# Ranks, expert choice, weight splits and the first slots' x in the attention half of an attention and mixture-of-experts kernel

## The chip, the core and the metric

The kernel runs on one core of a Trainium2 chip. The metric is device time in microseconds. Three runs of the kernel before took 625.83, 627.03 and 627.37 us; the median is 627.03 us.

## What is computed

Windowed attention (each position sees itself and the 63 before it) for 8 batches, 8 heads, 576 positions of 64 features gives 4608 tokens of 512 features. Each token then goes to one of 8 experts, and is scaled by its gate. All data is float32.

```python
scores = scale * np.matmul(q, k.transpose(0, 1, 3, 2))        # then mask, softmax
x = np.matmul(attn, v)  # as (4608, 512)

xn = x / (np.linalg.norm(x, axis=-1, keepdims=True) + 1e-06)
en = expert_emb / (np.linalg.norm(expert_emb, axis=-1, keepdims=True) + 1e-06)
logits = xn @ en.T / tau
expert_idx = np.argmax(logits, axis=1)
gate_w = probs[np.arange(N), expert_idx]                       # probs: softmax of logits
for e in range(E):
    mask = expert_idx == e
    h = np.maximum(x[mask] @ w1[e], 0.0)
    out[mask] = gate_w[mask, None] * (h @ w2[e])
```

## The kernel before

**Attention.** The 4608 tokens are 36 tiles of 128 rows. `stages(s)` (L520) is one turn of a software pipeline, called for s = 0 to 34: it computes the scores of tile s, the weights times values of tile s-2, and the transposed x and the logits of earlier tiles. The order of the work on each engine is the order in which this code stands; a wait on one instruction holds all that is queued behind it on that engine. In a stage ACT copies the scores out of PSUM (`own_scores`, L222), DVE puts the previous block's scores in (`all_scores`, L225) and takes maxima (L229), POOL subtracts them (`less_max`, L233), ACT takes the exponential (L236), PE transposes, ACT copies (L255), DVE and POOL mask the two halves (L258 and L261), PE multiplies with the values (L275 and L289), and DVE divides by the sums (`x_out`, L313 to L315).

**Routing.** Tiles form groups of four up to tile 28 and of two behind it (`GROUPS`, L33). Logits of a group land in PSUM (`misc`) and are copied beside x into the group's rows in SBUF (`four_out`, L361; L545; `logits_out`, L378). `choose(G)` (L382) takes the first largest of the eight logits of each token in five DVE steps (L391 to L395), three stages behind the group's end: for the groups of four in stages 7, 11, 15, 19, 23, 27 and 31. Two stages later, in 9, 13, 17, 21, 25, 29 and 33, `ranks(G)` (L407) lets PE sum how many earlier tokens chose each expert, with matmuls of bfloat16 ones. `rank_rows` (L440) then adds on DVE each expert's first row in the table (`at`: a constant, or `late0`, `late1` behind the cuts at tiles 20 and 32), multiplies with the choice, sums over experts and converts: the row in which the token's x goes. `place(T)` (L459) is the put: POOL issues an indirect DMA (L462) that writes the tile's rows into the table `xs` in DRAM, one in most stages.

**Slots.** Behind the attention, `step(g)` works through slots of 128 rows of one expert, two to a full group, with both layers in three float32r products of split operands: high part by ACT, rest by DVE or POOL. The first four slots are expert 0's earliest tokens, known before the attention ends. `load_x(a)` (L750) reads slot a's rows from `xs` with four DMAs on SP's queue into `xb`; for slots 0 and 1 it stands behind stage 30, behind that stage's put. `x_turned` (L763) transposes blocks of 32 on DVE (L770, four rows `x4`), `x_hi` (L779) rounds on ACT (L781), `x_lo` (L783) subtracts on POOL (L785). `x_parts` does the three in a row; for slots 0 and 1 behind stages 32 and 33.

**Weights.** Expert 0's w1 is loaded during the attention in eight halves of `w1raw` (L508), by stages 8, 10, 15, 18, 21, 24, 26 and 28. `wsplit` (L513) names the stages at whose end a half is split: ACT rounds it (L600), DVE subtracts (L601), stages 13, 15, 20, 23, 26, 28, 30 and 32. Halves of w2 are loaded in stages 29 to 33 (L512).

**The end of the attention.** The last tile and the first slots' first layer are interleaved by hand (L1082 to L1227): `layer1(0, f)` on PE between the last stages' work, the last ranks, `load_x(2)` and `load_x(3)`, then `slot_rows` (L652), a chain of small DVE steps that finds the expert and first row of every later slot, and the loads that depend on it.

Lines that the change touches and the prediction names are given with the numbers of the kernel before.

Of the kernel before, what the change touches and what calls it, by code (L numbers as in the profile page):

```python
# [9 lines left out]
F32 = mybir.dt.float32  # L10
# [5 lines left out]
ALU = mybir.AluOpType  # L16
# [5 lines left out]
P = 128  # L22
B, H, S, D = 8, 8, 576, 64
N, DM, DF, E = 4608, 512, 1024, 8
# [12 lines left out]
CUTS = 20, 32  # L37
# [18 lines left out]
K_ID, K_OWN, K_PREV, K_SEL, K_E, K_DESC, K_P, K_F, K_SL, K_U = 0, 128, 256, 384, 448, 456, 464, 465, 473, 476  # L56
# [27 lines left out]
def attention_moe(ctx, tc, q, k, v, emb, tau, w1, w2, kc, kt, out):  # L84
    nc = tc.nc
    ctx.enter_context(tc.manual_schedule())
    const = ctx.enter_context(tc.tile_pool(name="const", bufs=1))
# [53 lines left out]
    upper = const.tile([P, P], BF16, name="upper")  # L141
    ones = const.tile([P, P], BF16, name="ones")
    half = const.tile([P, 1], F32, name="half")
    embT = ap.tile([P, 4, 32], F32, name="embT", bufs=1)
    xs = dram.tile([TBL, ROW], F32, name="xs")

# [27 lines left out]
    def load_k(T, engine=nc.sync):  # L174
        if T < NT:
            engine.dma_start(kT[:, T % RK * KT:(T % RK + 1) * KT], k[T])
# [195 lines left out]
    def in_rows(G):  # L372

        return x_rows(*GROUPS[G])[:, :, C_LOG:C_LOG + E]
# [6 lines left out]

    def choose(G):  # L382

        L = in_rows(G)
        a, b = GROUPS[G]
        n = b - a
        m = ap.tile([P, n, 1], F32, name="m")
        c8 = ap.tile([P, n, E], F32, name="c8")
        oh = ohs[G] = ap.tile([P, n, E], BF16, name="oh")
        sh = [P, n, E]  # L390
        nc.vector.reduce_max(out=m, in_=L, axis=AX.X)  # L391
        nc.vector.tensor_tensor(out=c8, in0=L, in1=m.to_broadcast(sh), op=ALU.is_equal)
        nc.vector.tensor_tensor(out=c8, in0=c8, in1=cs[:, K_DESC:K_DESC + E].unsqueeze(1).to_broadcast(sh), op=ALU.mult)
        nc.vector.reduce_max(out=m, in_=c8, axis=AX.X)
        nc.vector.tensor_tensor(out=oh, in0=c8, in1=m.to_broadcast(sh), op=ALU.is_equal)  # L395
# [11 lines left out]
    def ranks(G):  # L407

        a, b = GROUPS[G]
        n = b - a  # L410
        rank[G] = rkb[0][:, 64:128].rearrange("p (a g e) -> p a g e", a=2, e=E)[:, G % 2, :n]
        nc.tensor.matmul(rank[G], lhsT=upper, rhs=ohs[G], start=True, stop=False)
        for i in range(1, n):
            nc.tensor.matmul(rank[G][:, i:], lhsT=ones, rhs=ohs[G][:, i - 1:i].to_broadcast([P, n - i, E]), start=False, stop=False)
        for i in range(4):
            nc.tensor.matmul(rank[G], lhsT=ones, rhs=before[G][:, i:i + 1].to_broadcast([P, n, E]), start=False, stop=i == 3)

    late = [const.tile([P, E], F32, name=f"late{i}") for i in range(len(CUTS))]
    shift = [const.tile([P, 1], F32, name=f"shift{i}") for i in range(len(CUTS))]
# [20 lines left out]
    def rank_rows(G):  # L440
        a, b = GROUPS[G]
        n = b - a
        rk = ap.tile([P, n, E], F32, name="rk")
        at = [cs[:, K_E:K_E + E], *late][sum(a >= cut for cut in CUTS)]
        nc.vector.tensor_tensor(out=rk, in0=rank.pop(G), in1=at.unsqueeze(1).to_broadcast([P, n, E]), op=ALU.add)
        yield
        nc.vector.tensor_tensor(out=rk, in0=rk, in1=ohs.pop(G), op=ALU.mult)
        yield
        pos = ap.tile([P, n], F32, name="pos")
        nc.vector.reduce_sum(out=pos, in_=rk, axis=AX.X)  # L450
        yield
        rks[G] = ap.tile([P, n], I32, name="pi")
        nc.vector.tensor_copy(rks[G], pos)
        yield
# [4 lines left out]
    def place(T):  # L459

        i = T - GROUPS[OF[T]][0]
        d = nc.gpsimd.indirect_dma_start(  # L462
            out=xs[:, :], out_offset=bass.IndirectOffsetOnAxis(ap=rks[OF[T]][:, i:i + 1], axis=0),
            in_=xr.pop(T), in_offset=None, bounds_check=TBL - 1, oob_is_err=False)
        d = getattr(d, "ins", d)
        for o in firsts:
            tc.declare_no_dep(d, o, reason="later tokens' places are behind the early slots")
        for o in puts:
            tc.declare_no_dep(d, o, reason="no two tokens share a place")
        puts.append(d)  # L470
# [39 lines left out]
    for i, s0 in enumerate((29, 30, 30, 31, 31, 32, 32, 33)):  # L510
        c, h = divmod(i, 2)
        wsteps.setdefault(s0, []).append(lambda c=c, h=h: nc.sync.dma_start(out=w2raw[c][:, h], in_=w2v[0, :, c, h]))  # L512
    wsplit = {s0: (i // 2, slice(i % 2 * 512, i % 2 * 512 + 512)) for i, s0 in enumerate((13, 15, 20, 23, 26, 28, 30, 32))}  # L513

    def warm(n, to=back):

# [3 lines left out]
    def stages(s):  # L520

        def there(d):
            return 0 <= s - d < NT

        def ending(d):
            return [G for G, (a, b) in enumerate(GROUPS) if b + d == s]

        def turned():
            if there(1):
                attn_transposes(s - 1)  # L530
                attn_copy(s - 1)

        scores(s)
        if s < 3:
            warm(12, misc)
        own_scores(s)
        if there(4) and s - 4 >= 28:
            logits(s - 4)
        four = [G for G in ending(3) if len(range(*GROUPS[G])) == 4]
        for G in ending(3):  # L540
            if G in four:
                logits_four(G)
                four_copy(G)
            else:
                nc.scalar.copy(in_rows(G), plv[:, G % 2, :GROUPS[G][1] - GROUPS[G][0]])  # L545
        load_q(s + RQ)
        if there(2):
            values_other(s - 2)
        load_v(s + RV - 3)
        for f in wsteps.get(s, ()):  # L550
            f()
        if s > 3:
            turned()
        if there(3):
            x_transposes(s - 3)
        for G in four:
            four_back(G)
        due = [G for G, (a, b) in enumerate(GROUPS) if s == (b + 5 if b - a == 4 else b + 4)]
        for G in due:
            if len(range(*GROUPS[G])) == 4:  # L560
                ranks(G)
        if there(2):
            values_mine(s - 2)
        all_scores(s)
        maxima(s)
        if s < 3:
            warm(12, misc)
        if there(3):
            xT_evac(s - 3)
        for G in four:  # L570
            four_out(G)
        less_max(s)
        if there(3):
            squares(s - 3)
        load_k(s + RK - 1, nc.scalar)
        if s > 3:
            attn_prev(s - 1)
            attn_own(s - 1)
        if there(2):
            x_out(s - 2)  # L580
        if 0 < s <= 3:
            turned()
            attn_prev(s - 1)
            attn_own(s - 1)
        for G in due:
            if len(range(*GROUPS[G])) == 2:
                ranks(G)
            ranks_out(G)
        for G, (a, b) in enumerate(GROUPS):
            for T in range(a, b):  # L590
                if s == (T + 9 if b - a == 4 else b + 4):
                    place(T)
        for G in ending(3):
            choose(G)
            tokens(G)
            count(G)
        exponentials(s)
        if s in wsplit:
            c, at = wsplit[s]
            nc.scalar.copy(w1h[c][:, at], w1raw[c][:, at])  # L600
            nc.vector.tensor_tensor(out=w1l[c][:, at], in0=w1raw[c][:, at], in1=w1h[c][:, at].bitcast(F32), op=ALU.subtract)  # L601
        if 1 <= s < 7:
            blanks(s - 1)
# [159 lines left out]
    def x_turned(a):  # L763

        b = xb.pop(a)
        xt[a] = take("xt")
        o = xt[a].rearrange("p (c t i) -> p t c i", c=4, i=32)
        bv = b.rearrange("p (t c j) -> p t c j", t=4, j=32)
        for k in range(4):
            nc.vector.transpose(o[:, k], bv[:, k])  # L770
# [8 lines left out]
    def x_hi(a):  # L779
        xh, xl, t = x_half(a)  # L780
        nc.scalar.copy(xh, t)  # L781

    def x_lo(a, eng=nc.gpsimd):  # L783
        xh, xl, t = x_half(a)
        eng.tensor_tensor(out=xl, in0=t, in1=xh.bitcast(F32), op=ALU.subtract)  # L785

    def x_parts(a):
        x_turned(a)
        x_hi(a)
        x_lo(a)  # L790
# [256 lines left out]
    nc.vector.memset(ones, 1.0)  # L1047
    nc.vector.memset(low, -BIG / 64)
    nc.vector.memset(half, 0.5)
    nc.scalar.copy(shift[0], half)  # L1050
    nc.vector.memset(embT, 0.0)
    nc.vector.memset(before[0], 0.0)
# [10 lines left out]
    for t in range(NT - 1):  # L1063
        stages(t)
        if t == 0:
            nc.vector.tensor_copy(upper, xbuf[2][:, :P])
        if t == 1:
            expert_norms()
        if t == 2:
            expert_emb()  # L1070
        if t == 3:
            expert_emb_T()
        if t == CUTS[0] + 4:
            sum_counts(CUTS[0])
            begin_late(0, counts("early"))
        if t == 30:
            load_x(0)
            load_x(1)
        if t in (32, 33):
            x_parts(t - 32)  # L1080

    stage_t.close()  # L1082
    rkb[0] = misc
# [207 lines left out]
```

## Time and profile before

| what | us |
| --- | --- |
| median of three runs | 627.03 |
| the profiled execution | 627.08 |
| its span, first to last instruction | 625.2 |
| PE (TensorE) matmul busy in the span | 595.9 |
| DVE (VectorE) busy | 425.4 |
| ACT (ScalarE) busy | 355.2 |
| POOL (GpSimd) busy | 232.5 |

The profile is one execution. Busy time of an engine is the time in which one of its instructions ran; an instruction that waits is not busy, and the row of it gives in brackets how long its engine had been idle and what ended that (`<-` and the engine and line, or the DMA). In `out<-in` names, buffer numbers are left out. A matmul's weight load is an engine of its own (PEld). The mean granted clock of PE is 0.991 of full speed.

### The profile page before, as it was taken

The numbers are of one execution on the slowest core, as the hardware profiler recorded it, in microseconds if no ns is written. First come the engines' busy times: TensorE is split into PE (matmuls) and PEld (weight loads), VectorE is DVE, ScalarE is ACT, GpSimd is POOL, SyncE is SP. The second block draws the span as 40 slices with busy tenths as digits, with TensorE's granted clock in tenths as the row PEclk, the third lists the DMA queues.
The fourth block names the chain that finished last, engine by engine and source line by source line (L and its number), as shares of the span: only waits on it lengthen the run. The fifth ranks groups of instructions, "written<-read, shape, count | busy, mean of one in ns | idle before, by whom it ended". The sixth has DMA issues, their size and how long they took to land. (4 is left out here: it accounts for less than half of the span.)

```text
span 625.2 us, 17780 instructions
## 1 busy us (share of the span) xinstructions
PE 595.9 (95%) x6836; PEld 531.6 (85%) x6836; DVE 425.4 (68%) x882; ACT 355.2 (57%) x566; POOL 232.5 (37%) x224
## 2 busy tenths in 40 slices
PE   8898989888999899999999999999999999999995
PEld 8777877777899699889988999899889998998884
DVE  2778888887786656675566776656766676657622
ACT  2666767666541446566466664645676466536542
POOL 1567787777732133213103431142023331222011
PEclk9999999999899899999999999999999999999998
DMA  8877888886346578866786897849778877776241
GB/s 291 265 218 244 268 264 273 268 273 190 119 133 204 149 242 291 258 209 231 243 273 219 276 302 238 275 145 322 246 244 243 276 270 226 232 261 221 106 148 37
DMA packets 85789, 143.75 MB, mean 230 GB/s; under 512 B 15797, under 2 KB 36021, under 8 KB 85696
## 3 DMA queue, kind: packets, MB, share of 16 engines
q1 hardware_dynamic: 74560, 112.87, 57.6%
q0 software_dynamic: 6000, 19.18, 7.8%
q10 hardware_dynamic: 5136, 10.49, 5.2%
q8 instruction: 55, 0.90, 0.6%
q14 instruction: 38, 0.31, 0.2%
HBM read 123.23 MB, written 20.05 MB: 229 GB/s over the span
## 5 line engine op out<-in xcount | busy, mean ns | idle before, releaser
L887 PE MATMUL ph<-xh,w1h 128*128 128x256 f32 x576 | 162.4, 282 | 0.0
L887 PE MATMUL ph<-xh,w1l 128*128 128x256 f32 x576 | 161.9, 281 | 0.0
L887 PE MATMUL ph<-xl,w1h 128*128 128x256 f32 x576 | 161.7, 281 | 0.0
L957 POOL DMA_INDIRECT out<-o,rest x39 | 50.5, 1294 | 222.1 <-ACT o L956 208.9
L947 PE MATMUL po<-w2l,hh 128*128 128x512 f32 x312 | 122.2, 392 | 2.6 <-DVE w2l L161 2.6
L947 PE MATMUL po<-w2h,hh 128*128 128x512 f32 x312 | 122.7, 393 | 0.0
L947 PE MATMUL po<-w2h,hl 128*128 128x512 f32 x312 | 122.4, 392 | 0.0
L901 DVE SCALAR_TENSOR_TENSOR hl<-ph,hh 128x512 fp32r<-128x512 f32 x78 | 53.3, 689 | 92.8 <-ACT hh L897 92.7
L161 DVE TENSOR_TENSOR w2l<-w2raw,w2h 128x1024 fp32r<-128x1024 f32 x80 | 94.7, 1220 | 24.7 <-ACT w2h L158 23.0
L887 PEld LDWEIGHTS ph<-xl,w1h 128*128 128x128 f32 x576 | 108.6, 189 | 0.9
L887 PEld LDWEIGHTS ph<-xh,w1h 128*128 128x128 f32 x576 | 108.4, 188 | 0.9
L887 PEld LDWEIGHTS ph<-xh,w1l 128*128 128x128 f32 x576 | 108.5, 188 | 0.0
L158 ACT CAST w2h<-w2raw 128x1024 fp32r<-128x1024 f32 x80 | 81.5, 1048 | 40.0 <-PE po L947 32.0
L161 DVE TENSOR_TENSOR w1l<-w1raw,w1h 128x1024 fp32r<-128x1024 f32 x76 | 88.5, 1225 | 9.4 <-ACT w1h L158 9.1
L785 POOL TENSOR_TENSOR xl<-xt,xh 128x512 fp32r<-128x512 f32 x37 | 47.8, 1292 | 101.2 <-ACT xh L781 101.2
L897 ACT ACTIVATE hh<-ph 128x512 fp32r<-128x512 f32 x78 | 46.0, 594 | 54.4 <-PE ph L887 47.8
L158 ACT CAST w1h<-w1raw 128x1024 fp32r<-128x1024 f32 x76 | 73.9, 1047 | 0.0
L947 PEld LDWEIGHTS po<-w2l,hh 128*128 128x128 f32 x312 | 58.9, 189 | 14.7 <-DVE w2l L161 3.1
L947 PEld LDWEIGHTS po<-w2h,hl 128*128 128x128 f32 x312 | 58.8, 189 | 12.7
L947 PEld LDWEIGHTS po<-w2h,hh 128*128 128x128 f32 x312 | 58.7, 188 | 11.6
L781 ACT CAST xh<-xt 128x512 fp32r<-128x512 f32 x39 | 24.2, 619 | 62.9 <-DVE xt L770 62.3
L233 POOL TENSOR_TENSOR sm<-sm,st 128x512 f32<-128x512 f32 x36 | 37.5, 1041 | 37.8 <-DVE st L229 30.1
(193 smaller groups left out, 834.3 us busy)
## 6 DMA issues: line engine op xcount, KB each, us to landing
w2raw<-in_w SPq DMA_DIRECT2D x76, 512.0 KB
w1raw<-in_w SPq DMA_DIRECT2D x72, 512.0 KB
xb<-xs SPq DMA_DIRECT2D x156, 64.0 KB
v<-in_v SPq DMA_DIRECT2D x36, 260.0 KB
qT<-in_q SPq DMA_DIRECT2D x36, 256.0 KB
kT<-in_k ACTq DMA_DIRECT2D x32, 256.0 KB
w1raw<-in_w SPq DMA_DIRECT2D x8, 256.0 KB
w2raw<-in_w SPq DMA_DIRECT2D x8, 256.0 KB
```

Of the source, the lines that this page charges most:

```text
L158: nc.scalar.copy(hi[c], raw[c])
L161: eng.tensor_tensor(out=lo[c], in0=raw[c], in1=hi[c].bitcast(F32), op=ALU.subtract)
L233: nc.gpsimd.tensor_tensor(out=t, in0=t, in1=st.pop(T).unsqueeze(2).to_broadcast([P, 8, WIN]), op=ALU.subtract)
L781: nc.scalar.copy(xh, t)
L785: eng.tensor_tensor(out=xl, in0=t, in1=xh.bitcast(F32), op=ALU.subtract)
L887: nc.tensor.matmul(o, lhsT=ww[c][:, f * P:(f + 1) * P], rhs=xx[:, c, :n], start=(c == 0 and i == 0), stop=(c == 3 and i == 2))
L897: nc.scalar.activation(hh, ph[g, part], AF.Relu)
L901: nc.vector.scalar_tensor_tensor(out=hl, in0=ph.pop((g, part)), scalar=0.0, in1=hh.bitcast(F32), op0=ALU.max, op1=ALU.subtract)
L947: nc.tensor.matmul(po[a], lhsT=xx[:, f, at], rhs=ww[f // 2][:, f % 2], start=(f == 0 and i == 0), stop=(f == 7 and i == 2))
L957: d = nc.gpsimd.indirect_dma_start(out=out, out_offset=bass.IndirectOffsetOnAxis(ap=tok, axis=0), in_=o, in_offset=None, bounds_check=N - ...
```

## The change

1. `ranks` gets one more matmul, in float32: a row of ones (`one`, a new tile of one partition) times the row of first table rows (`at`) of one partition, added to the same PSUM sums. `rank_rows` loses its addition; its product reads PSUM.
2. `choose` reads the logits in PSUM and no longer their copy in SBUF. The copy remains, since it is written to the table with x.
3. `wsplit`: the fourth to eighth halves are split in stages 22, 24, 26, 28 and 30, and no longer in 23, 26, 28, 30 and 32.
4. `x_parts` of slots 0 and 1 is taken apart: `x_turned` behind stages 31 and 32, `x_hi` in stages 32 and 33 before the exponential, `x_lo` there behind the puts.

```diff
+    one = const.tile([1, P], F32, name="one")
...
     def choose(G):
 
-        L = in_rows(G)
         a, b = GROUPS[G]
         n = b - a
+        L = plq[:, G % 2, :, :E] if n == 4 else plv[:, G % 2, :n]
...
         for i in range(4):
-            nc.tensor.matmul(rank[G], lhsT=ones, rhs=before[G][:, i:i + 1].to_broadcast([P, n, E]), start=False, stop=i == 3)
+            nc.tensor.matmul(rank[G], lhsT=ones, rhs=before[G][:, i:i + 1].to_broadcast([P, n, E]), start=False, stop=False)
+        at = [cs[:, K_E:K_E + E], *late][sum(a >= cut for cut in CUTS)]
+        nc.tensor.matmul(rank[G], lhsT=one, rhs=at[:1].unsqueeze(1).to_broadcast([1, n, E]), start=False, stop=True)
...
-        at = [cs[:, K_E:K_E + E], *late][sum(a >= cut for cut in CUTS)]
-        nc.vector.tensor_tensor(out=rk, in0=rank.pop(G), in1=at.unsqueeze(1).to_broadcast([P, n, E]), op=ALU.add)
-        yield
-        nc.vector.tensor_tensor(out=rk, in0=rk, in1=ohs.pop(G), op=ALU.mult)
+        nc.vector.tensor_tensor(out=rk, in0=rank.pop(G), in1=ohs.pop(G), op=ALU.mult)
...
-    wsplit = {s0: (i // 2, slice(i % 2 * 512, i % 2 * 512 + 512)) for i, s0 in enumerate((13, 15, 20, 23, 26, 28, 30, 32))}
+    wsplit = {s0: (i // 2, slice(i % 2 * 512, i % 2 * 512 + 512)) for i, s0 in enumerate((13, 15, 20, 22, 24, 26, 28, 30))}
...
         load_k(s + RK - 1, nc.scalar)
+        if s in (32, 33):
+            x_hi(s - 32)
...
                 if s == (T + 9 if b - a == 4 else b + 4):
                     place(T)
+        if s in (32, 33):
+            x_lo(s - 32)
...
+    nc.vector.memset(one, 1.0)
...
-        if t in (32, 33):
-            x_parts(t - 32)
+        if t in (31, 32):
+            x_turned(t - 31)
```

What this makes of DVE's order from the end of stage 31 to stage 33 is shown below; line numbers of the change are its own (L225 is L226 there, L315 is L316, L770 is L774). First before, from the choice's last step in stage 31:

```order
L395 TENSOR_TENSOR oh<-c_2997,m 128x32
L225 COPY_PREDICATED sm<-cs,score 128x512
L229 TENSOR_REDUCE st<-sm 128x8
L258 TENSOR_TENSOR aM<-back,cs 128x512
L313 TENSOR_SCALAR sums<-pair 128x8
L314 RECIPROCAL sums<-sums 128x8
L315 TENSOR_TENSOR xr<-pair,sums 128x512
L601 TENSOR_TENSOR w1l_112<-w1raw,w1h_108 128x512
L770 STREAM_TRANSPOSE xt_224<-xb_218 128x4x32 x4
L225 COPY_PREDICATED sm<-cs,score 128x512
```

And the same place on DVE in the change:

```order
L396 TENSOR_TENSOR oh<-c_3001,m 128x32
L774 STREAM_TRANSPOSE xt_226<-xb_220 128x4x32 x4
L226 COPY_PREDICATED sm<-cs,score 128x512
L230 TENSOR_REDUCE st<-sm 128x8
L259 TENSOR_TENSOR aM<-back,cs 128x512
L314 TENSOR_SCALAR sums<-pair 128x8
L315 RECIPROCAL sums<-sums 128x8
L316 TENSOR_TENSOR xr<-pair,sums 128x512
L774 STREAM_TRANSPOSE xt_227<-xb_221 128x4x32 x4
L226 COPY_PREDICATED sm<-cs,score 128x512
```

The split has left stage 32, slot 0's turn stands ahead of that stage and slot 1's in the place of slot 0's. The second place is DVE behind stage 24's division (L315), where the first cut's counts are turned into `late0`; before:

```order
L315 TENSOR_TENSOR xmore<-pair,sums 128x512
L428 COPY early<-rkb 128x8
L433 TENSOR_SCALAR shift_122<-early 128x1
L434 TENSOR_SCALAR shift_122<-shift_122 128x1
L435 COPY late_120<-cs 128x8
L436 COPY late_120<-shift_122 128x1
L225 COPY_PREDICATED sm<-cs,score 128x512
```

In the change, at that place:

```order
L316 TENSOR_TENSOR xmore<-pair,sums 128x512
L605 TENSOR_TENSOR w1l_112<-w1raw,w1h_108 128x512
L431 COPY early<-rkb 128x8
L436 TENSOR_SCALAR shift_123<-early 128x1
L437 TENSOR_SCALAR shift_123<-shift_123 128x1
L438 COPY late_121<-cs 128x8
L439 COPY late_121<-shift_123 128x1
L226 COPY_PREDICATED sm<-cs,score 128x512
```

A weight split now stands between the division and the counts. The third place is ACT in stages 32 and 33; before, from stage 32's exponential:

```order
L236 ACTIVATE sm<-sm 128x512
L600 CAST w1h_108<-w1raw 128x512
L781 CAST xh_221<-xt_224 128x4x128
L222 COPY sm<-score 128x512
L545 COPY xr<-misc 128x2x8
```

In the change, from slot 0's rounding to the same copy:

```order
L785 CAST xh_223<-xt_226 128x4x128
L237 ACTIVATE sm<-sm 128x512
L223 COPY sm<-score 128x512
L545 COPY xr<-misc 128x2x8
L256 COPY aM<-back 128x512
```

The weight's rounding is gone from stage 32, and slot 0's rounding stands ahead of the exponential and no longer between it and the next score copy.

## The prediction

> **What bounds the kernel now.** I read the page first, then busy time by stretches, then the row-by-row timeline of VectorE, GpSimd and ScalarE between 40 and 190 us. The first row below is from the page (busy time of each engine). The next three are stretches of the span: start and end, length, then busy us of PE, PE's weight loads, DVE, ACT and POOL, then the granted clock.
>
> ```profile
> PE 595.9 (95%) x6836; PEld 531.6 (85%) x6836; DVE 425.4 (68%) x882; ACT 355.2 (57%) x566; POOL 232.5 (37%) x224
> ...
> 120.00:140.00 20.00, 17.48 (x496) 15.18 (x496) 17.27 (x40) 14.17 (x32) 15.42 (x16) 1.00 0.85 270
> 158.00:160.00 2.00, 2.00 (x14) 1.64 (x10) 1.74 (x10) 0.09 (x1) 1.13 (x2) 0.50 0.12 41
> 163.00:200.00 37.00, 36.85 (x484) 33.69 (x482) 30.45 (x124) 14.70 (x27) 17.48 (x24) 1.00 0.41 138
> ```
>
> PE's 95% hides two regimes. Up to about 162 us (attention) PE and DVE are both busy and both wait; from 163 us PE is full, so what is gained before that is kept only if the start of the full part moves. Every edit lies in or near the first regime. There the 36 stages turn around one loop. The next rows (start, duration, engine, line, and in brackets the idle time before it) show the plain stage 8. I count a stage from one L225 to the next.
>
> ```profile
> 42.16 0.72 DVE L225 COPY_PREDICATED sm<-cs,score 128x512 f32<-128x512 uint32 x1
> 43.75 1.04 POOL L233 TENSOR_TENSOR sm<-sm,st 128x512 f32<-128x512 f32 x1 [1.19 <-DVE st L229]
> 44.83 0.63 ACT L236 ACTIVATE sm<-sm 128x512 f32<-128x512 f32 x1 [0.54 <-POOL sm L233]
> 45.37 0.57 ACT L222 COPY sm<-score 128x512 f32<-128x512 f32 x1
> 45.97 0.74 DVE L225 COPY_PREDICATED sm<-cs,score 128x512 f32<-128x512 uint32 x1 [0.66 <-ACT sm L222]
> ```
>
> From L225 over the maximum, POOL's subtraction, the exponential and the next score copy it is 3.81 us, and DVE has 0.66 us to spare: **3.81 us is the floor of a stage**. Extra DVE work beyond the spare time, or ACT work between L236 and L222, lengthens it. These are the L225 rows at the ends of the stages that the change touches:
>
> ```profile
> 98.16 0.73 DVE L225 COPY_PREDICATED sm<-cs,score 128x512 f32<-128x512 uint32 x1
> 102.43 0.73 DVE L225 COPY_PREDICATED sm<-cs,score 128x512 f32<-128x512 uint32 x1
> 106.55 0.74 DVE L225 COPY_PREDICATED sm<-cs,score 128x512 f32<-128x512 uint32 x1 [0.97 <-ACT sm L222]
> 111.70 0.72 DVE L225 COPY_PREDICATED sm<-cs,score 128x512 f32<-128x512 uint32 x1
> 115.69 0.73 DVE L225 COPY_PREDICATED sm<-cs,score 128x512 f32<-128x512 uint32 x1
> 129.24 0.72 DVE L225 COPY_PREDICATED sm<-cs,score 128x512 f32<-128x512 uint32 x1
> 133.68 0.73 DVE L225 COPY_PREDICATED sm<-cs,score 128x512 f32<-128x512 uint32 x1
> 142.71 0.73 DVE L225 COPY_PREDICATED sm<-cs,score 128x512 f32<-128x512 uint32 x1
> 147.25 0.71 DVE L225 COPY_PREDICATED sm<-cs,score 128x512 f32<-128x512 uint32 x1
> 153.74 0.73 DVE L225 COPY_PREDICATED sm<-cs,score 128x512 f32<-128x512 uint32 x1 [1.17 <-ACT sm L222]
> 161.05 0.73 DVE L225 COPY_PREDICATED sm<-cs,score 128x512 f32<-128x512 uint32 x1 [1.17 <-ACT sm L222]
> ```
>
> So stage 21 (with ranks) takes 4.27, stage 22 4.12, stage 23 (choice and weight split) 5.15, stage 24 (with the counts of the first cut) 3.99, stage 28 (split alone) 4.44, stage 31 (choice) 4.54, stage 32 6.49 and stage 33 7.31.
>
> **Ranks and choices.** The first row is POOL's product of that time, the next two are the two rank steps of stage 21; then three groups (count, then total and mean ns).
>
> ```profile
> 100.77 1.27 POOL L261 TENSOR_TENSOR aM<-aM,cs 128x512 f32<-128x512 f32 x1
> 101.23 0.18 DVE L445 TENSOR_TENSOR rk<-rkb,cs 128x32 f32<-128x32 f32 x1
> 101.44 0.65 DVE L447 TENSOR_TENSOR rk<-rk,oh 128x32 f32<-128x32 f32 x1
> ...
> L369 PE MATMUL misc<-embT,xT 128*64 128x8 f32 x128 | 5.1, 205 | 0.1
> L392 DVE TENSOR_TENSOR c<-xr,m 128x32 f32<-128x32 f32 x5 | 2.2, 434 | 0.2
> L392 DVE TENSOR_TENSOR c<-xmore,m 128x32 f32<-128x32 f32 x2 | 1.3, 654 | 0.1
> ```
>
> L445 reads PSUM and ran through L261 in 0.18 us. L447, with both inputs in SBUF, lasted until 102.09, just after L261's end at 102.04: it was held. The change leaves one product that reads PSUM, so L445's slot (0.21) and the hold (0.65-0.18) go, 0.68 us of DVE; the floor allows 4.27-3.81 = 0.46. Against it stands one more f32 matmul on PE ahead of L289, whose sums DVE takes next. This shape is not in the trace; the nearest row is L369 at 0.205 us, and the ends are 0 (it overlaps its neighbours) and 0.2. I take 0.1 and -0.3 us a stage for 9, 13, 17, 21, 25 and 29: **-1.8** (ends -2.8 and 0).
>
> In a choice L391 and L392 now read PSUM. L392 means 434 and 654 ns against 0.18 unheld, so about five of seven were held. But the next step, L393, still has both inputs in SBUF and comes 0.21 earlier, so it meets the same POOL product: only 0.2 is saved where there was a hold. In stages 11, 15 and 27: **-0.6** (ends -1.4 and 0).
> By the Trainium skill, page "SBUF — State Buffer", section "Who interferes with whom", a VectorE instruction with two SBUF inputs contends with a GpSimd instruction that reads SBUF, and one with at most one SBUF input outside its two-port modes does not. L445 at 0.18 and L447 at 0.65 under one L261 agree. It speaks against the second edit: a reader who counts the whole hold as saved would write -1.4 for those three stages, while by the rule it passes on to L393 and -0.6 stays.
>
> **Weight splits.** A split costs a plain stage 4.44-3.81 = 0.63, because L600 stands between the exponential and the next score copy. Stage 22 receives one: +0.6. Stage 23 loses one: it becomes a choice alone like stage 31's 4.54, less 0.2, so 5.15 to 4.3: -0.8. Stage 24 receives one, and there the shift steps from L428 on stand behind it on DVE:
>
> ```profile
> 114.76 0.16 DVE L428 COPY early<-rkb 128x8 f32<-128x8 f32 x1
> ```
>
> From L428 to L225 at 115.69 is 0.93, now behind a stage of 4.44: 5.37 against 3.99, +1.4. Together **+1.2** (0.2 less if a hold in the shift steps goes). Ranks that end earlier let the put behind them start earlier; I take 0.1 for that. Stages 0 to 30 come to -1.8-0.6+1.2-0.1 = **-1.3**.
>
> **Stages 31 to 33.** What stands there now, with the loads of slots 0 and 1 on SP's queue, and what that queue moved from 145.4 to 149.1 us:
>
> ```profile
> 145.48 4.35 SPq L755 DMA_DIRECT2D xb<-xs  x8
> ...
> q1 hardware_dynamic: 572, 0.26, 33.7%
> ...
> 149.69 0.69 DVE L315 TENSOR_TENSOR xr<-pair,sums 128x512 f32<-128x512 f32 x1
> 151.08 0.69 DVE L601 TENSOR_TENSOR w1l<-w1raw,w1h 128x512 fp32r<-128x512 f32 x1 [0.69 <-ACT w1h L600]
> 151.69 0.89 DVE L770 STREAM_TRANSPOSE xt<-xb 128x128 f32<-128x128 f32 x4
> ```
>
> In stage 32 DVE ends L315 at 150.38, waits for the split, turns slot 0 until 152.58; ACT rounds that, and only then copies the scores for which L225 waits until 153.74. All of it is in a row; moving it apart should gain. But in the change DVE reaches slot 0's turn right behind stage 31's choice, near 147.0 on this clock. Each load is 64 KB, so four are 0.26 MB: slot 0 is there at **149.1**. DVE stands two microseconds, and L225 of stage 32 is queued behind: 149.1+0.89 = 150.0 for 147.25, **+2.8**. The load itself waits for stage 30's put, which the change leaves in place.
>
> Stage 32 is then L225 to L315's end, 150.38-147.25 = 3.13, and slot 1's turn of 0.89: 4.0 for 6.49, **-2.5**. Slot 0's rounding runs on ACT while POOL subtracts. Stage 33 loses the turn, but POOL is the bound now:
>
> ```profile
> 155.34 1.04 POOL L233 TENSOR_TENSOR sm<-sm,st 128x512 f32<-128x512 f32 x1 [0.77 <-DVE st L229]
> 158.86 1.02 POOL L462 DMA_INDIRECT xs<-xr,pi  x1 [1.25 <-issue]
> 160.61 1.27 POOL L785 TENSOR_TENSOR xl<-xt,xh 128x512 fp32r<-128x512 f32 x1 [0.22 <-ACT xh L781]
> 162.65 1.04 POOL L233 TENSOR_TENSOR sm<-sm,st 128x512 f32<-128x512 f32 x1 [0.77 <-ACT sq L324]
> ```
>
> A stage with subtraction, product, put and L785 is 1.04+1.27+1.02+1.27 and about 0.5 of gaps and slower puts, 5.1 us, against 4.0. The subtraction that starts 1.6 behind its L225 (155.34-153.74) starts 2.7 behind it in stage 33; the exponential and score copy follow, and DVE's third choice step waits for POOL's product: 5.5 for 7.31, **-1.8**. In stage 34 it is again 1.1 later. Of that, POOL's puts pass something on:
>
> ```profile
> 173.53 0.98 POOL L462 DMA_INDIRECT xs<-xr,pi  x1 [0.77 <-issue]
> 174.82 1.25 POOL L462 DMA_INDIRECT xs<-xr,pi  x1 [0.30 <-ACT xT L337]
> ...
> 184.91 0.89 DVE L770 STREAM_TRANSPOSE xt<-xb 128x128 f32<-128x128 f32 x4 [0.43 <-DMA xb<-xs]
> ...
> L947 PE MATMUL po<-w2l,hh 128*128 128x512 f32 x312 | 122.2, 392 | 2.6 <-DVE w2l L161 2.6
> ```
>
> The put at 173.53 had 0.77-0.30 = 0.47 to spare, so 0.6 of the 1.1 reaches slot 3's rows, for which L770 waits at 184.91. From there the slot table, the next loads and the weight rests run to PE's one wait of 2.6 us in L947; behind it PE is full. What is gained at 185 us is gained at the end, less this **+0.6**.
>
> **Sum.** -1.3+2.8-2.5-1.8+0.6 = **-2.2**. The profiled execution took 627.08 us (span 625.2 and 1.9 around it), 0.05 above the median of 627.03, so the forecast is **624.9 us**. The clock of 0.50 at 158 to 160 us can come back in stage 33 and would cost some 0.5.
>
> **Rivals.**
> - *Slot 0's rows are there in time.* Then stage 31 pays only the turn, 0.89-0.2 = 0.7 in place of 2.8: 622.8. For it: they are asked for a whole stage earlier than now used. Against it: 149.1 is read from the queue's bytes, and nothing moves the load.
> - *The small DVE steps are not on the path* (the added matmul and the holds eat them): -1.8-0.6-0.1 become 0, 627.4, no measurable change. For it: stage 22 has 0.97 of idle DVE; against it: L225 of stages 22 and 24 began without idle time.
> - *Slower.* If slot 0's load waits for the put of stage 31 in place of stage 30's, the rows come a stage of 4.5 us (147.25-142.71) later, all of it behind DVE's queue: 629.4. It turns to a loss once the rows land later than 149.1+2.2 = 151.3. For it: SP takes 4.35 us to issue the eight loads, and they read what the puts write. Against it: the put of stage 31 stands behind the load in the program.
>
> **How the numbers follow.** 0.52 for the forecast, 0.20 for the first rival, 0.20 for the second, 0.08 for slower. A measurement here tells about 0.3%, 1.9 us, from no change. The forecast's own spread is 623.3 to 626.4 by the ends above, so some 0.31 of its 0.52 lies below 625.1: faster 0.51, same 0.39, slower 0.10. The range takes in the first two rivals with that spread: 622.0 to 628.0.
>
> **What would show it.** Right: L225 of stage 32 behind a DVE wait of about 2 us for xb; stage 24 above 5 us, stages 21 and 25 near 3.9; the rank product at 0.18 and L393 held in its place; stage 32 near 4.0. Wrong: no wait for xb in stage 31 (then the first rival), rank stages still at 4.27 (the second), or a PE gap in L947 that does not move with stage 34.

## The result and the profile after

| | before | after |
| --- | --- | --- |
| median of 20 runs each | 627.64 us | 630.94 us |
| range of the runs | 625.01 to 630.91 | 628.68 to 634.22 |
| the profiled execution (its span) | 627.08 (625.2) | 634.22 (632.4) |

The ratio is 1.0057, 95% interval 1.0042 to 1.0071: the change costs 3.6 us by it (3.3 between the medians). The prediction of 624.9 us, 622.0 to 628.0, was wrong in sign. The profiled execution is the slowest of its twenty, so its trace shows more loss (7.2 us of span) than the median; a second trace, of the fastest execution of another set, stands beside it below.

The end of the attention, in the timeline of the changed kernel on DVE (start, duration, engine, line; in brackets the idle time before it and what ended that):

```profile
142.65 0.73 DVE L226 COPY_PREDICATED sm<-cs,score 128x512 f32<-128x512 uint32 x1
...
146.83 0.19 DVE L396 TENSOR_TENSOR oh<-c,m 128x32 bf16<-128x32 f32 x1
149.75 0.89 DVE L774 STREAM_TRANSPOSE xt<-xb 128x128 f32<-128x128 f32 x4 [2.72 <-DMA xb<-xs]
150.56 0.69 DVE L226 COPY_PREDICATED sm<-cs,score 128x512 f32<-128x512 uint32 x1
...
154.40 0.70 DVE L226 COPY_PREDICATED sm<-cs,score 128x512 f32<-128x512 uint32 x1
...
158.12 1.02 DVE L453 CAST pi<-pos 128x4 int32<-128x4 f32 x1
159.06 0.16 DVE L392 TENSOR_REDUCE m<-misc 128x2 f32<-128x16 f32 x1
159.25 0.17 DVE L393 TENSOR_TENSOR c<-misc,m 128x16 f32<-128x16 f32 x1
...
160.05 0.73 DVE L226 COPY_PREDICATED sm<-cs,score 128x512 f32<-128x512 uint32 x1
...
170.96 0.73 DVE L226 COPY_PREDICATED sm<-cs,score 128x512 f32<-128x512 uint32 x1
```

Stage 31 takes 7.91 us, 32 takes 3.84, 33 takes 5.65, all near the prediction's 7.3, 4.0 and 5.5. Stage 34 takes 10.91. The prediction's sum had nothing for it but the +0.6 that the puts pass on; before, it took 165.41-161.05 = 4.36:

```profile
165.41 0.73 DVE L225 COPY_PREDICATED sm<-cs,score 128x512 f32<-128x512 uint32 x1
```

PE's rows say what happened there, first in the change (the last is its wait in the first slots' second layer), then before:

```profile
151.31 0.89 PE L216 MATMUL score<-kT,qT 64*64 64x128 f32 x24 [1.76 <-DVE sm L226]
...
159.57 0.60 PE L370 MATMUL misc<-embT,xT 128*64 128x8 f32 x15 [2.11 <-DVE c L393]
...
218.28 0.50 PE L951 MATMUL po<-w2l,hh 128*128 128x512 f32 x1 [2.46 <-DVE w2l L162]
```

```profile
154.53 1.10 PE L215 MATMUL score<-kT,qT 64*64 64x128 f32 x32 [1.56 <-DVE sm L225]
155.56 0.64 PE L369 MATMUL misc<-embT,xT 128*64 128x8 f32 x16
...
210.10 0.50 PE L947 MATMUL po<-w2l,hh 128*128 128x512 f32 x1 [2.63 <-DVE w2l L161]
```

**The choice of stage 33 now reads the logits in `misc`, and PE's logits of stage 34 (L370) write into `misc`.** PE waits for the second choice step (L393, to 159.42 us), with the values, transposes and scores of the last stages queued behind it. Before, only the copy out of PSUM stood there, and L369 followed the scores without a wait (155.56). The two do not touch the same columns: by the code (L366, L387) the choice's group has the half `G % 2` = 1 of its part of `misc`, and the next logits go into half 0. So the matmul does not wait for the place that it overwrites, but for the reading of any part of `misc`; no run keeps the halves apart. The next lines are stretches of the span of the changed kernel (start and end, length, busy us of PE, its weight loads, DVE, ACT, POOL, the granted clock):

```profile
158.00:160.00 2.00, 0.43 (x15) 0.46 (x16) 1.83 (x7) 1.02 (x2) 1.19 (x2) 1.00 0.07 27
160.00:162.00 2.00, 2.00 (x46) 1.91 (x45) 1.46 (x3) 0.33 (x1) 1.97 (x2) 0.77 0.31 107
162.00:174.00 12.00, 12.00 (x126) 10.95 (x125) 5.23 (x15) 3.58 (x7) 7.15 (x12) 0.50 0.20 76
174.00:176.00 2.00, 2.00 (x55) 1.53 (x57) 0.04 (x1) 1.43 (x4) 1.35 (x3) 0.82 0.00 0
163.00:200.00 37.00, 36.89 (x498) 33.14 (x497) 22.53 (x84) 14.09 (x28) 15.53 (x23) 0.84 0.26 83
```

Behind the wait PE runs at half clock for 13.65 us in which it is busy without a break. Behind the wait in L951 the two spans are alike again: 632.4-218.28 = 414.1 and 625.2-210.10 = 415.1. So the difference arises between 142 and 218 us.

A second execution of the same kernel, from another set (e12 below; first DVE, then PE). At 632.32 us it is the fastest of its seven, 0.5 us above the median of the kernel before in that set:

```profile
143.26 0.73 DVE L226 COPY_PREDICATED sm<-cs,score 128x512 f32<-128x512 uint32 x1
...
150.98 0.89 DVE L774 STREAM_TRANSPOSE xt<-xb 128x128 f32<-128x128 f32 x4 [3.22 <-DMA xb<-xs]
151.80 0.69 DVE L226 COPY_PREDICATED sm<-cs,score 128x512 f32<-128x512 uint32 x1
...
155.63 0.69 DVE L226 COPY_PREDICATED sm<-cs,score 128x512 f32<-128x512 uint32 x1
...
161.76 0.72 DVE L226 COPY_PREDICATED sm<-cs,score 128x512 f32<-128x512 uint32 x1
...
168.94 0.73 DVE L226 COPY_PREDICATED sm<-cs,score 128x512 f32<-128x512 uint32 x1
```

```profile
161.29 0.64 PE L370 MATMUL misc<-embT,xT 128*64 128x8 f32 x16 [1.26 <-DVE c L393]
```

Both waits are there again (3.22 and 1.26 us), but only one stretch of half clock, 3.41 us long and over before the second wait; stage 34 takes 7.18. The two waits belong to the kernel, the long stretch at half clock to some of its executions: three more of the first twenty have a mean clock as low as the profiled one (0.983 for 0.984, the others 0.986 to 0.993).

The ranks, in the groups of the changed kernel (count, total and mean ns):

```profile
L453 DVE CAST pi<-pos 128x4 int32<-128x4 f32 x7 | 2.7, 386 | 0.2
...
L419 PE MATMUL rkb<-cs,one 1*128 1x32 f32 x10 | 2.0, 282 | 0.0
...
L447 DVE TENSOR_TENSOR rk<-rkb,oh 128x32 f32<-128x32 f32 x7 | 1.3, 181 | 0.0
```

The product L447 is free of its hold (181 ns for 478), but the cast two steps behind it takes 386 ns for 170: there it meets POOL's product, for 1.02 us in stage 33 at 158.12 above. By the Trainium skill, page "SBUF — State Buffer", section "Who interferes with whom", copies and casts can enter a two-port mode and then contend with GpSimd; the trace agrees, and the prediction used that section for the product alone. The f32 matmul shows as two rows of 0.28 us a group, against the 0.1 that the prediction took. In stage 9 DVE's first division step waits for PE's values behind it, in the change and before:

```profile
47.94 0.17 DVE L314 TENSOR_SCALAR sums<-pair 128x8 f32<-128x8 f32 x1 [0.57 <-PE pair L290]
```

```profile
48.33 0.17 DVE L313 TENSOR_SCALAR sums<-pair 128x8 f32<-128x8 f32 x1 [0.23 <-PE pair L289]
```

### The profile page after: what moved, and what is told of

Same layout as the page of the kernel before. It is cut to its first block, busy times and chain, and to the rows that moved or that the text cites. A ratio compares the mean times of both kernels' runs of the same rounds, so it can differ in the third digit from the quotient of the medians.

```text
span 632.4 us, 17818 instructions
## 1 busy us (share of the span) xinstructions
PE 602.6 (95%) x6858; PEld 538.0 (85%) x6858; DVE 423.3 (67%) x872; ACT 355.4 (56%) x566; POOL 232.7 (37%) x224
## 5 line engine op out<-in xcount | busy, mean ns | idle before, releaser
L951 PE MATMUL po<-w2l,hh 128*128 128x512 f32 x312 | 122.4, 392 | 2.5 <-DVE w2l L162 2.5
L951 PE MATMUL po<-w2h,hh 128*128 128x512 f32 x312 | 122.7, 393 | 0.0
L951 PE MATMUL po<-w2h,hl 128*128 128x512 f32 x312 | 122.5, 393 | 0.0
L951 PEld LDWEIGHTS po<-w2l,hh 128*128 128x128 f32 x312 | 58.9, 189 | 14.6 <-DVE w2l L162 2.9
L951 PEld LDWEIGHTS po<-w2h,hl 128*128 128x128 f32 x312 | 59.0, 189 | 12.6
L951 PEld LDWEIGHTS po<-w2h,hh 128*128 128x128 f32 x312 | 58.8, 189 | 11.7
L785 ACT CAST xh<-xt 128x512 fp32r<-128x512 f32 x39 | 24.1, 619 | 59.0 <-DVE xt L774 58.3
```

The source lines that it names most:

```text
L951: nc.tensor.matmul(po[a], lhsT=xx[:, f, at], rhs=ww[f // 2][:, f % 2], start=(f == 0 and i == 0), stop=(f == 7 and i == 2))
```

## The experiments

Eighteen runs were made, in five sets of three or four, each set on one chip. The median of the kernel before was 631.9, 631.6, 631.8, 626.9 and 631.9 us in them, so only ratios to it are compared. Between sets even these differ for the change: 1.0057 in the set of the result, 1.0092 in e12. Before against itself (e15), and e10 and e14 run again, stayed within 0.1%. A difference between sets that has the change on one side tells nothing below some 0.35%. "31 to 34" is the time from the L225 (L226) of stage 31 to that of stage 35 in the run's one trace: 22.70 us before, 28.31 after.

| run | what it is | ratio | 95% interval | 31 to 34, us |
| --- | --- | --- | --- | --- |
| e1 | change, choice from SBUF | 1.0059 | 1.0040 to 1.0078 | 25.8 |
| e2 | before, choice from PSUM | 1.0011 | 0.9988 to 1.0034 | 27.3 |
| e3 | change, slots as before | 1.0061 | 1.0037 to 1.0084 | 25.5 |
| e4 | change, ranks as before | 1.0036 | 1.0023 to 1.0050 | 25.9 |
| e5 | change, both waits gone | 1.0130 | 1.0104 to 1.0156 | 27.6 |
| e6 | change, PE kept busy | 1.0067 | 1.0043 to 1.0091 | 25.7 |
| e7 | before, ranks on PE | 1.0008 | 0.9989 to 1.0028 | 24.0 |
| e8 | before, slots of the change | 1.0020 | 1.0009 to 1.0032 | 25.1 |
| e9 | before, roundings one stage on, rest of slot 1 on DVE | 0.9948 | 0.9929 to 0.9967 | 20.8 |
| e10 | change, SBUF, slots as e9 | 0.9968 | 0.9951 to 0.9986 | 20.4 |
| e11 | before, splits moved | 0.9986 | 0.9967 to 1.0004 | 23.8 |
| e12 | the change again | 1.0092 | 1.0070 to 1.0113 | 25.7 |
| e13 | change, slots as e9 | 1.0001 | 0.9983 to 1.0019 | 24.1 |
| e14 | e9 with splits moved | 0.9945 | 0.9923 to 0.9967 | 19.4 |
| e15 | before again | 1.0006 | 0.9988 to 1.0024 | 24.7 |
| e16 | e14, ranks on PE to stage 29 | 0.9952 | 0.9936 to 0.9969 | 19.9 |
| e17 | e10 again | 0.9961 | 0.9942 to 0.9980 | 19.4 |
| e18 | e14 again | 0.9955 | 0.9937 to 0.9972 | 19.4 |

**One edit undone.** The first theory was that the wait of stage 34 and its half clock are the whole loss.

```diff
-        L = plq[:, G % 2, :, :E] if n == 4 else plv[:, G % 2, :n]
+        L = in_rows(G)
```

> The changed kernel, but the choice reads the logits from their copy in SBUF again (second edit undone, all others kept). Theory A, the loss sits in stage 34: TensorE's logits of the next tile wait until the choice of stage 33 has read the logits in PSUM, TensorE idles some 2 us there and its clock then falls to 0.50 for some 13 us. Then this kernel has no wait of TensorE on c in stage 34, no long stretch at 0.50 behind it, and the time is 3 to 5 us below the 630.94 of the changed kernel: 626 to 628. Theory B, the loss is the wait for slot 0's rows in stage 31 and the added matmul in the ranks: then this kernel stays at 630 to 632, since both are still in it.

```diff
-        if t in (31, 32):
-            x_turned(t - 31)
+        if t in (32, 33):
+            x_parts(t - 32)
```

(and `x_hi`, `x_lo` out of `stages`)

> The changed kernel with the fourth edit undone: the turn and the rounding of slots 0 and 1 stand in stages 32 and 33 as before. Theory A: the wait of TensorE in stage 34 stays, since the choice still reads PSUM; the wait of 2.7 us for slot 0's rows goes and stages 32 and 33 are long again: 629.5 to 632. Theory B: the stall of stage 31 is the loss, and without it the time is that of before or better, 626 to 628.

```diff
-        nc.tensor.matmul(rank[G], lhsT=one, rhs=at[:1].unsqueeze(1).to_broadcast([1, n, E]), start=False, stop=True)
...
+        nc.vector.tensor_tensor(out=rk, in0=rank.pop(G), in1=at.unsqueeze(1).to_broadcast([P, n, E]), op=ALU.add)
```

> The changed kernel with the first edit undone: place bases are added on VectorE again, no f32 matmul in the ranks. Theory A: 630 to 632, the loss of stage 34 stays. Theory B, where the f32 matmuls (2 rows of 0.28 us in each of 11 groups) delay VectorE: 1 us or more below the changed kernel, 629 to 630. By the prediction's own term the first edit was worth -1.8, and this kernel would be 1.8 above the changed one.

1.0059, 1.0061 and 1.0036: undoing any one of these three edits leaves a loss of 0.4 to 0.6%, so none of them carries it alone, and theory A as it stood falls. e1 still has the wait for slot 0's rows (3.26 us), e3 the wait for the choice (1.84), e4 both.

**One edit alone.** Each is the matching piece of the diff, put into the kernel before.

> The kernel before, with the second edit alone: the choice reads the logits in PSUM. Theory A: TensorE's logits of stage 34 wait behind the second step of the choice of stage 33 (158.2 in the trace of before, its scores end at 155.6), so the loss appears without any other edit: 2 to 5 us above the kernel before, 629.5 to 632.5. Theory B (the edit only moves a hold on VectorE): 627 to 628, no change that can be measured.

> The kernel before with the first edit alone (place bases added by an f32 matmul on TensorE). The prediction's term: -1.8 us, a ratio of 0.997. Theory E, the f32 matmul shows as two rows of 0.28 us ahead of the values, and the hold passes on to the cast behind the product, so the edit gains nothing and costs some: 1.001 to 1.003, as the 0.2% between the changed kernel (1.0057) and the one without this edit (1.0036) suggests.

> The kernel before with the fourth edit alone (turn of slots 0 and 1 one stage earlier, roundings apart). The prediction's terms: +2.8-2.5-1.8+0.6 = -0.9 us, a ratio of 0.9986. Theory C, the wait of VectorE for slot 0's rows in stage 31 is a loss by itself (2.7 to 4 us there, TensorE idle behind it): 1.003 to 1.006. A DVE wait for xb ahead of the turn is in the trace in both.

> The kernel before with the third edit alone (weight splits in stages 22, 24 and 30 in place of 23 and 32). The prediction's terms: +0.6-0.8+1.4 = +1.2, less what stage 32 gains without its split (0.6, in the prediction part of -2.5): a ratio of 1.001. Rival, from the differences of the variants so far: 1.002 to 1.004.

1.0011, 1.0008, 1.0020 and 0.9986. Only the slots cost measurably by themselves; their wait for rows is 3.72 us in e8. The choice alone costs nothing that can be told, though PE's wait for it is there, longer than in the change:

```profile
160.59 0.64 PE L369 MATMUL misc<-embT,xT 128*64 128x8 f32 x16 [2.88 <-DVE c L392]
```

The ranks do not gain their 0.3% (0.997 lies outside the interval). The four sum to +0.25%, known to about 0.4%. The change costs 0.6 to 0.9%, and e3, which has three of them, 0.6%: 0.9% is clear of that sum, 0.6% is not. So it is likely, not certain, that the edits hinder each other. One place where they can is in the first trace of the change: the cast that the ranks leave to be held (1.02 us) stands right ahead of the choice for which PE now waits. That is argued, not shown; in e12 the cast is not held there.

**The clock.** Matmuls that nobody reads, meant for PE's three waits:

```diff
+        if s == 32:
+            warm(16, rkb[0][:, 256:])
         scores(s)
...
+        if s == 34:
+            warm(20, rkb[0][:, 256:])
         if there(4) and s - 4 >= 28:
             logits(s - 4)
...
+            if s == 33:
+                warm(8, rkb[0][:, 256:])
             values_other(s - 2)
```

> The changed kernel with idle-time matmuls of 128x128 bf16 on TensorE whose results nobody reads: 16 ahead of the scores of stage 32, 8 ahead of the values of stage 33, 20 ahead of the logits of stage 34, that is where TensorE waited 1.76, 0.75 and 2.11 us. They shorten no wait. Theory clock, the loss is mostly windows of 3.41 us at a clock of 0.50 that TensorE's idle time calls up: the clock time lost in a run (1 less its mean clock, by its span: 7.3 us for the changed kernel) falls below 5 and the ratio to before falls from 1.0057 to 1.001 to 1.003. Theory waits, the waits themselves are the loss: the ratio stays at 1.005 to 1.008.

The stretch where the change had half clock, in this kernel:

```profile
158.00:176.00 18.00, 17.16 (x351) 15.40 (x347) 13.07 (x34) 9.88 (x20) 15.13 (x21) 1.00 0.36 133
```

The clock is full there, and the clock time lost in a run falls to 5.2 us on average, about to the 5 that was expected (7.3 and 8.1 for the change in its two sets) and below the 6.3 of the kernel before in this set. The ratio stays at 1.0067, and stages 31 to 34 still take 3.0 us more than before. So the loss is there without extra half clock. Two limits: the sixteen matmuls ahead of stage 32's scores ran at 145.88 us, a stage too early for the wait for slot 0's rows, which stayed unfilled (1.97 us of idle PE at 153.82); and no run tells what the 44 matmuls cost by themselves, though in this trace the work behind the other 28 waits for DVE and not for them.

> The changed kernel once more, for a second trace of it: 1.004 to 1.007 of the kernel before. If the four windows at half clock behind stage 34 (160 to 174 us) belong to the change, they are there again; if their number hangs on where the windows fall, there are one to three, with the time nearer its median. The waits for slot 0's rows in stage 31 and for c in stage 34 are there in any case.

1.0092. Its trace, with one window of half clock, does not show this loss: it is that of the fastest execution, 632.32 us at a mean clock of 0.996, where the other six took 634.90 to 639.16 at 0.980 to 0.989. The kernel before took 629.75 to 636.35 in this set, 631.80 in the median. So an execution with both waits can do without most of the 0.92%. Over all executions of this set the clock time lost is 8.1 us for the change, 5.5 for the kernel before and 2.7 for e9, the fast variant below. So in this set the clock goes with the time, against what e6 shows. How the loss divides between the length of the waits and the clock stays open.

**Both waits gone.** Choice from SBUF, and slots 0 and 1 one stage later:

```diff
-        if s in (32, 33):
-            x_hi(s - 32)
+        if s in (33, 34):
+            x_hi(s - 33)
...
-            x_lo(s - 32)
+            x_lo(s - 33)
...
-        if t in (31, 32):
-            x_turned(t - 31)
+        if t in (32, 33):
+            x_turned(t - 32)
```

> The changed kernel without both of its new waits: the choice reads the copy in SBUF, and the turn of slot 0 stands at the end of stage 32, that of slot 1 at the end of stage 33 (roundings one stage behind). Ranks and splits as in the change. Theory C, either of the two waits alone costs the 3 us (each of the first four variants kept one of them and lost 0.1 to 0.6%): without both this kernel is at 0.996 to 1.001 of the kernel before. Theory D, the loss is spread in what stays (the f32 matmul in the ranks, the moved splits): it stays at 1.003 or above.

1.0130, the worst of all. Its PE timeline has the reason:

```profile
161.49 0.38 PE L891 MATMUL ph<-xh,w1h 128*128 128x256 f32 x1
167.90 0.58 PE L891 MATMUL ph<-xl,w1h 128*128 128x256 f32 x1 [6.04 <-POOL xl L789]
```

Layer 1 starts at 161.49 us (166.93 in the change), and then waits 6.04 us for slot 1's rest, which stood behind three puts on POOL in stage 34. So layer 1 does start earlier when both waits are gone, and the variant loses it at once. The next kernels give slot 1's rest to DVE, ahead of the puts:

```diff
         maxima(s)
+        if s == 34:
+            x_hi(1)
+            x_lo(1, nc.vector)
...
+        if s == 33:
+            x_hi(0)
...
+        if s == 33:
+            x_lo(0)
...
         if t in (32, 33):
-            x_parts(t - 32)
+            x_turned(t - 32)
```

> The kernel before with one thing moved: the turns of slots 0 and 1 stay in stages 32 and 33, but their roundings and rests move one stage on (slot 0: ScalarE and GpSimd in stage 33; slot 1: ScalarE and VectorE early in stage 34, ahead of the puts on GpSimd that made TensorE wait 6.04 us for xl in the fifth variant). Theory F: ScalarE's score copy no longer stands behind the rounding, so stages 32 and 33 take about 5 and 6 us in place of 6.5 and 7.3, layer 1 starts 2 to 4 us earlier and that stays to the end: a ratio of 0.993 to 0.997. Rival: what is gained in these stages is waited for again (for slot 1's rest, or for later rows), 0.999 or above.

> The same placement of slots 0 and 1 with the first and third edit of the change (f32 matmul in the ranks, splits moved) and the choice from SBUF. If those two edits cost what the variants so far say (0.1% and 0.2 to 0.3%), it stands 0.2 to 0.4% above the variant without them: 0.996 to 1.000. If they gain as the prediction had the ranks (-1.8 +1.2), it is 0.1% below that variant.

0.9948 and 0.9968: with this placement the kernel before gains 0.5%, and the change without the choice from PSUM beats before too. In the set of e12 (1.0092) the step from the change to e10 is worth 1.24% of 631.8 us, 7.8 us.

> The changed kernel with the slots placed as in the faster variants (turns in stages 32 and 33, roundings one stage on) and the choice still reading PSUM: it differs from the variant at 0.9968 in the choice's source alone. Theory A2: TensorE's wait for c in stage 34 (1.3 to 2.9 us in the traces so far) is a loss by itself, 1.000 to 1.004. Rival: the choice from PSUM saves its copy and costs nothing once slot 0 does not stall, 0.996 to 0.998.

> The fastest variant (0.9948) with the splits of the change, that is the variant at 0.9968 without the f32 matmul in the ranks. If the matmul costs what e4 against the changed kernel says (0.2%), this one is at 0.993 to 0.996. If ranks on TensorE gain as predicted (-1.8 us), it is at 0.999.

> The kernel before, once more: a ratio of 0.998 to 1.002, and a trace of it from the chip of the other two. Expected in it: 22 to 23 us from the L225 of stage 31 to that of stage 35, and none or one window of half clock between 150 and 175 us.

e13 is the change with nothing altered but the slots, and stands at 1.0001 where the change, in other sets, is at 1.0057 and 1.0092. **So the change gains 0.6 to 0.9% when slots 0 and 1 are placed as in e9.** That is not the price of the fourth edit: the kernel before gains 0.5% by the same placement, the edit alone cost 0.2%, and undoing it in the change (e3) gained nothing against 1.0057. The choice from PSUM is what separates e13 from e10 and e17 (0.9968 and 0.9961, in other sets), and, with the ranks, from e14 in its own set (0.9945): 0.3 to 0.6%. PE's wait for the choice is in the trace of e13:

```profile
156.21 0.82 PE L370 MATMUL misc<-embT,xT 128*64 128x8 f32 x16 [1.25 <-DVE c L393]
```

Not all of that step need be this wait, since DVE's rest of slot 1 was held in that trace too (last section). e14, the fastest of its set (622.77 us for 626.86), on DVE and then PE:

```profile
143.81 0.73 DVE L225 COPY_PREDICATED sm<-cs,score 128x512 f32<-128x512 uint32 x1
148.34 0.71 DVE L225 COPY_PREDICATED sm<-cs,score 128x512 f32<-128x512 uint32 x1
...
152.20 0.70 DVE L225 COPY_PREDICATED sm<-cs,score 128x512 f32<-128x512 uint32 x1
...
158.25 0.69 DVE L225 COPY_PREDICATED sm<-cs,score 128x512 f32<-128x512 uint32 x1
...
163.22 0.73 DVE L225 COPY_PREDICATED sm<-cs,score 128x512 f32<-128x512 uint32 x1
```

```profile
160.18 0.38 PE L894 MATMUL ph<-xh,w1h 128*128 128x256 f32 x1
```

Stages 32 and 33 take 3.86 and 6.05 with stage 31 at 4.53, and layer 1 starts at 160.18 us.

> Slots 0 and 1 placed as in the faster variants, splits moved, choice from SBUF; the f32 matmul of the ranks only in the groups of stages 9 to 29, and VectorE's addition again from stage 33 on. If the first edit costs because its last matmuls stand where TensorE is full, this one is about 1 us below the variant with all of them and 1 us below the one with none (stages 21 and 25 keep their 0.45 each): 0.992 to 0.994. If its gain in the stages is lost elsewhere, it is level with the variant with none.

> The same with the f32 matmul in all groups, as run before at 0.9968: 0.995 to 0.999, and 0.1 to 0.3% above the variant without it. By the prediction's term it would be 0.3% below.

> The same with no f32 matmul in the ranks, as run before at 0.9945: 0.992 to 0.997.

0.9952, 0.9961 and 0.9955 on one chip: the ranks on PE neither gain nor cost anything that can be told, with or without their last matmuls.

## Why the prediction was wrong

- **Stages 32 and 33: right.** -2.5 and -1.8 were forecast; the profile of the change has 3.84-6.49 = -2.65 and 5.65-7.31 = -1.66. e9 and e14 show that the gain is real and can be kept.
- **Stage 31: right in kind, too small.** DVE stands for slot 0's rows as predicted. But their landing at 149.1 us was read from the queue's bytes; DVE got them at 149.75, 4.35 us behind the first issue at 145.40 (4.97 in e12, 5.55 in e8, on their own clocks). +2.8 became 7.91-4.54 = +3.4, and in e12 and e8 stage 31 took 8.54 and 9.13. PE stood still behind it (1.76 us at 151.31). The whole slots edit, -0.9 by the prediction's terms, cost 0.20% alone (+1.3 us).
- **Stage 34: the step that failed.** The working of the choices went through VectorE alone: what L391 and L392 save there when they read PSUM. That the edit also adds a wait, PE's next logits behind the choice's last reading of `misc`, was put at nothing: it was not in the sum, nor among the rivals. It is 2.11 us of idle PE with the last stages queued behind it, 10.91-4.36 = +6.55 with the half clock of that execution. e13 beside e10, e14 and e17 puts the edit at 0.3 to 0.6%; e1, which undid it with slot 0's wait left in, gained nothing against 1.0057 and 0.3% against 1.0092, and e2, the edit alone, has 2.88 us of it at 1.0011. So the wait is shown; its price in the change stays open.
- **The sum of the edits** was the second thing that failed. Alone they measured +0.5 (ranks), +0.7 (choices), +1.3 (slots) and -0.9 us (splits), together +1.6, known to about 2.4, where the prediction had -2.2. What else there is in the measured 3.6 (5.8 in e12) shows only with edits combined, and its cause stays open.
- **Ranks: mis-sized, -1.8 against nothing.** Stages 21 and 25 fell by 0.45 each, to 3.82 and 3.80, as forecast (4.27 to about 3.9), and 29 by 0.11. But 9, 13 and 17 stayed where they were within 0.02. In stage 9 DVE waits 0.57 us for PE's values where it waited 0.23 before: the added matmul costs some 0.34 us there, not 0.1. The rest of the hold went on to the cast. e17 and e18 differ by 0.06%, each known to 0.18%.
- **Choices: -0.6 against nothing.** Stages 11, 15 and 27 changed by +0.17, 0.00 and -0.22. Part of the hold did pass on to the next step, as the prediction said: the third step means 289 ns for 196, where the second had 434 and 654 and now has 192.
- **Splits: stage by stage right.** Stages 22, 23 and 24 changed by +0.65, -0.85 and +1.18 (forecast +0.6, -0.8, +1.4). Alone the edit is at 0.9986, no change that can be told; stage 32, which loses a split, takes 5.10 in e11 for 6.49.
- **Stages 0 to 30** came to 142.65-7.71 = 134.94 us from the first L226, for 133.83 before: +1.1 for -1.3. Of the difference 0.74 is stage 19 (5.37 for 4.63), where one score matmul came 0.70 us late without a wait that the trace names; with kernels that have none of these edits, stage 19 is at 4.62 in e15 and at 4.99 in e9, so it is not the change's.
- **Behind stage 34** the profile loses 2.6 us more up to the end of the wait in L951 (218.28-170.96 = 47.32 for 210.10-165.41 = 44.69). The prediction expected +0.6 there from puts passed on. Half clock up to 175 us would make up most of it; that is argued, not shown.

Of the rivals, the one on the slower side had the right place (DVE in stage 31) but another cause, a load that waits for the next put; no run shows that, the rows are merely later than read. The second rival, for which ranks and choices come to nothing, had these two right. Nearly every sign that the prediction named for being right came: the wait for `xb` (2.72 us), stages 21, 24, 25 and 32, the product at 0.18. None of them looked at PE's queue in stage 34.

## What to carry to other kernels

An edit that lets an engine read PSUM directly, to save a copy, gives the buffer back later: ask which matmul writes there next, into whatever part of it, and what is queued behind it on TensorE. A step that is moved earlier to relieve one engine has to be checked against when its input lands and against the queue of whatever reads its output: the work on the same two slots cost 0.2% in one order (e8), gained 0.5% in another (e9), and kept TensorE waiting for 6 us in a third (e5). Edits whose waits stand within the same few stages have to be measured together: alone the four summed to +1.6 us, together they cost 3.6 and 5.8.

## What was not expected of the hardware

- In these traces every stretch at a granted clock of 0.50 between 140 and 190 us lasts a multiple of 3.41 us: 3.41 before and in e3, e7 and e12, 13.65 after, 10.24 in e4, e5, e11 and e15, 6.83 in e1, e2, e8 and e13, twice 3.41 in e16 and e18, none in e6, e9, e10, e14 and e17. The kernel before has 3.41 in one execution and 10.24 in another, so a single trace says little about it. The Trainium skill, page "TensorE: Matmul & The Clock Gate", section "What's actually happening", has a window of 3413 ns, and the traces agree with that length. By the same section of the Trainium skill the full clock comes back after at least one busy window. Here one was not enough: the profile has PE busy for 12.00 of 12.00 us at 0.50.
- A VectorE instruction can be held through two GpSimd instructions in a row. In e13, DVE and then POOL:

```profile
159.45 2.64 DVE L792 TENSOR_TENSOR xl<-xt,xh 128x512 fp32r<-128x512 f32 x1 [0.45 <-ACT xh L788]
```

```profile
159.28 1.03 POOL L234 TENSOR_TENSOR sm<-sm,st 128x512 f32<-128x512 f32 x1
160.28 1.25 POOL L262 TENSOR_TENSOR aM<-aM,cs 128x512 f32<-128x512 f32 x1
```

The same rest takes 0.68 us in e14, e17 and e18. By the Trainium skill, page "SBUF — State Buffer", section "Who interferes with whom", the instruction that comes first keeps the shared ports for its whole length; here the second one kept them too.
- The kernel before differs by 0.8% between the sets of e13 and e16 (626.9 and 631.9 us), as much as the change is worth. Both carry the same chip number, so the number does not tell them apart.
